# Chunk-selected attention and an MLP: scores of two heads in two halves of the PE rows, a separate mask matmul, and x centred in place of W1

## The chip, the cores and the metric

The kernel runs on one core of a Trainium2 chip. The metric is the device time of one launch in microseconds (us); lower is better. TensorE is called PE below, VectorE DVE, ScalarE ACT, GpSimd POOL and SyncE SP.

## The reference

Four batches, eight heads, 768 positions, head size 64; then a layer norm and an MLP over 512 channels with 2048 hidden ones.

```python
k_min, k_max = min and max of k over chunks of 32 positions
ub = sum over d of max(q * k_min, q * k_max)          # a bound for each query and chunk
ub = where(query's chunk >= chunk, ub, -1e9)
top_chunks = the 6 chunks with the highest ub
mask = (chunk of key in top_chunks) & (query >= key)
attn = softmax(where(mask, q @ k.T / 8, -1e9)) @ v
x = attn, heads side by side                          # 4 x 768 x 512
xn = (x - mean(x)) / sqrt(var(x) + 1e-6) * g_ln
out = x + relu(xn @ w_ch1) @ w_ch2
```

## The kernel before

**Units of work.** A pair `g` is two heads of one batch; there are 16 pairs, four to a batch. Tiles have 128 partitions; the 768 positions are six tiles. `load_qk` and `load_v` fetch a pair (q and k in f32 on SP's queue, v on POOL's, cast to f16).

**Preparation.** `prep_q` (L201) transposes q with six f32 PE transposes into a PSUM tile, casts it to f16 as `qh` on ACT, and forms the rest `ql` and the two parts `rh`, `rl` of its positive half on DVE. It copies the two heads' halves of `qh` into `QA` and `QB`. `prep_k` (L222) transposes k, takes minima and maxima over chunks on DVE, copies k on ACT into `KA` and `KB`, and builds `BD` for the bounds. `bounds` (L243) makes 20 matmuls of 96 columns, `select` (L257) finds the chunks with `max` (DVE's eight largest) and writes a 0/1 matrix `MN` of the chunks that are not selected, and `mask_t` (L274) transposes it and copies it into the other half of `QA` and `QB`.

**Scores.** The stationary operand `KA` holds 64 rows of k of one head and, in the other 64 rows, the matrix `RT`, which has -61440 where a row's chunk holds the key. `QA` has q in the same 64 rows and the transposed `MN` in the others. So one K=128 matmul (L297) gives scores and mask at once; `KB`, `QB` serve the other head with the halves exchanged. `score_bin` (L287) fills one PSUM bank `mm`, and ACT's exp (L306) empties it into `pt`. `diag` (L310) multiplies the diagonal blocks by a triangle on DVE. `values` (L317) multiplies by v with a column of ones, and `normalise` (L331) divides on DVE into `x_all`.

**MLP.** `w1_scale` multiplies W1 by the layer norm's gain, `w1_mean` computes its column means with 16 matmuls, and `w1_center` subtracts them, so that x needs no centring ahead of the product. `x_t` (L341) transposes x by pair. `stats` (L355) takes mean and variance of a row. `mlp1` (L376) and `mlp2` (L391) are the two products; the 1/std is applied at the end (L403), with the residual.

**Order.** The pieces are handed over in an order written out by hand: each has a due time `at(t, ...)` in units of one pair, and they are sorted by it (L410 to L454). The framework's scheduler then sets each engine's final queue. The MLP of a batch is spread over the four pairs that follow; that of the last batch has nothing beside it. PSUM: one two-bank `tr` tile, one `trh`, two `sm`, and three `mm` banks, which scores, W1 means and both MLP products share.

Of the kernel before, what the change touches and what calls it, by code (L numbers as in the profile page):

```python
# [9 lines left out]
ACTF = mybir.ActivationFunctionType  # L10
# [8 lines left out]
def kernel(  # L19
# [12 lines left out]

    nc = tc.nc
# [4 lines left out]
    CH = 32  # L38
    NCH = S // CH
    NT = S // P  # L40
    HP = H // 2
# [13 lines left out]
    SB0 = S - P  # L55
# [3 lines left out]
    ldp = ctx.enter_context(tc.tile_pool(name="ldp", bufs=3))  # L59
    vap = ctx.enter_context(tc.tile_pool(name="vap", bufs=4))  # L60
    prp = ctx.enter_context(tc.tile_pool(name="prp", bufs=2))
    smp = ctx.enter_context(tc.tile_pool(name="smp", bufs=2))
    ptp = ctx.enter_context(tc.tile_pool(name="ptp", bufs=3))
    xp = ctx.enter_context(tc.tile_pool(name="xp", bufs=2))
    htp = ctx.enter_context(tc.tile_pool(name="htp", bufs=1))
    outp = ctx.enter_context(tc.tile_pool(name="outp", bufs=3))

    PSUM = bass.MemoryType.PSUM
    ps_t = ctx.enter_context(tc.tile_pool(name="ps_t", bufs=1, space=PSUM))
# [4 lines left out]
    q_r = q.rearrange("b h (t p) d -> b p t h d", p=P)  # L74
    k_r = k.rearrange("b h (t p) d -> b p t h d", p=P)
    v_r = v.rearrange("b h (t p) d -> b p t h d", p=P)
    out_r = out.rearrange("b (t p) n -> b t p n", p=P)

    pieces = []

    def at(t, fn):
        pieces.append((t, len(pieces), fn))
# [4 lines left out]
    Lmask = const.tile([P, P], F16, name="Lmask", tag="Lmask")  # L87
    causb = const.tile([P, NT - 1, NCH], F32, name="causb", tag="causb")
    RT = const.tile([P, S], F16, name="RT", tag="RT")
    mean_w = const.tile([P, P], F16, name="mean_w", tag="mean_w")  # L90
    mhalf = const.tile([P, NT], F32, name="mhalf", tag="mhalf")
    NR = 3
    QA = [ring.tile([P, S], F16, name=f"QA{i}", tag=f"QA{i}") for i in range(NR)]
    QB = [ring.tile([P, S], F16, name=f"QB{i}", tag=f"QB{i}") for i in range(NR)]
    KA = [ring.tile([P, S], F16, name=f"KA{i}", tag=f"KA{i}") for i in range(NR)]
    KB = [ring.tile([P, S], F16, name=f"KB{i}", tag=f"KB{i}") for i in range(NR)]

    BD = [ring.tile([P, 2, 2, 2, NCH], F16, name=f"BD{i}", tag=f"BD{i}") for i in range(2)]
    MN = [ring.tile([P, NT - 1, P], F16, name=f"MN{i}", tag=f"MN{i}") for i in range(2)]

    def consts_first():
        make_identity(nc, ident_f)
        nc.vector.tensor_copy(ident_h, ident_f)
        for i in range(2):
            nc.vector.memset(BD[i], 0.0)
        for i in range(2):
            nc.vector.memset(MN[i], 0.0)
        nc.gpsimd.memset(causb, 0.0)
        nc.gpsimd.affine_select(
            out=causb, in_=causb, compare_op=ALU.is_ge, fill=CAUSAL,  # L110
            base=P, pattern=[[P, NT - 1], [-CH, NCH]], channel_multiplier=1,
        )
        nc.gpsimd.memset(RT, 0.0)
        for r0 in (0, 64):
            rr = RT[r0:r0 + NCH, :]
            nc.gpsimd.memset(rr, -NEGM)
            nc.gpsimd.affine_select(
                out=rr, in_=rr, compare_op=ALU.is_ge, fill=0.0,
                base=0, pattern=[[1, S]], channel_multiplier=-CH,
            )  # L120
            nc.gpsimd.affine_select(
                out=rr, in_=rr, compare_op=ALU.is_ge, fill=0.0,
                base=CH - 1, pattern=[[-1, S]], channel_multiplier=CH,
            )
        nc.gpsimd.memset(Lmask, 1.0)
        nc.gpsimd.affine_select(
            out=Lmask, in_=Lmask, compare_op=ALU.is_ge, fill=0.0,
            base=0, pattern=[[1, P]], channel_multiplier=-1,
        )
        nc.gpsimd.memset(mhalf, -0.5)  # L130
        nc.gpsimd.memset(mean_w, 1.0 / DM)

    def consts_ring(i):
        nc.vector.tensor_copy(KA[i][64:P, :], RT[64:P, :])
        nc.vector.tensor_copy(KB[i][0:64, :], RT[0:64, :])
        nc.vector.memset(QA[i][64:P, 0:P], 0.0)
        nc.vector.memset(QB[i][0:64, 0:P], 0.0)
# [5 lines left out]
    w1mean = const.tile([P, HID], F16, name="w1mean", tag="w1mean")  # L143
    w1_r = moe_w_ch1.rearrange("(kt p) n -> p kt n", p=P)
    w2_r = moe_w_ch2.rearrange("(kt p) n -> p kt n", p=P)

    def w1_load(kt):
        if kt == 0:
            nc.sync.dma_start(gstr, moe_g_ln.rearrange("(kt p) -> p kt", p=P))
        nc.gpsimd.dma_start(w1b[:, kt, :], w1_r[:, kt, :])  # L150
# [3 lines left out]

    def w1_scale(kt):
        nc.vector.tensor_scalar(
            w1b[:, kt, :], w1b[:, kt, :], gstr[:, kt:kt + 1], None, op0=ALU.mult,
        )

    def w1_mean(j):  # L160
        mp = ps_m.tile([P, 512], F32, name="mm", tag="mm")
        for kt in range(KT1):
            nc.tensor.matmul(
                mp, mean_w, w1b[:, kt, 512 * j:512 * j + 512], start=(kt == 0), stop=(kt == KT1 - 1),
            )
        nc.scalar.copy(w1mean[:, 512 * j:512 * j + 512], mp)

    def w1_center(kt):
        nc.vector.tensor_tensor(w1b[:, kt, :], w1b[:, kt, :], w1mean, ALU.subtract)  # L169
# [13 lines left out]
    def load_qk(g):  # L183
        b, hp = divmod(g, HP)
        qn = ldp.tile([P, NT, 2, D], F32, name="qn", tag="qn")
        kn = ldp.tile([P, NT, 2, D], F32, name="kn", tag="kn")
        for hh in range(2):
            nc.sync.dma_start(qn[:, :, hh, :], q_r[b, :, :, 2 * hp + hh])
        for hh in range(2):
            nc.sync.dma_start(kn[:, :, hh, :], k_r[b, :, :, 2 * hp + hh])  # L190
        st[g].update(qn=qn, kn=kn)

    def load_v(g):
        b, hp = divmod(g, HP)
        va = vap.tile([P, 2, NT, 80], F16, name="va", tag="va")
        for hh in range(2):
            nc.gpsimd.dma_start(va[:, hh, :, 0:D], v_r[b, :, :, 2 * hp + hh])  # L197
        nc.gpsimd.memset(va[:, :, :, D:D + 1], 1.0)
        st[g].update(va=va)

    def prep_q(g):  # L201
        qn = st[g]["qn"]
        pst = ps_t.tile([P, S], F32, name="tr", tag="tr")
        for t in range(NT):
            nc.tensor.transpose(pst[:, t * P:(t + 1) * P], qn[:, t, :, :], ident_f)  # L205
        qh = prp.tile([P, S], F16, name="qh", tag="qh")
        ql = prp.tile([P, SB0], F16, name="ql", tag="ql")
        rh = prp.tile([P, SB0], F16, name="rh", tag="rh")
        rl = prp.tile([P, SB0], F16, name="rl", tag="rl")
        nc.scalar.activation(qh, pst, ACTF.Copy, scale=QS)  # L210
        nc.vector.scalar_tensor_tensor(  # L211
            ql, pst[:, P:S], QS, qh[:, P:S], op0=ALU.mult, op1=ALU.subtract,
        )
        nc.vector.tensor_scalar_max(rh, qh[:, P:S], 0.0)
        nc.vector.scalar_tensor_tensor(  # L215
            rl, qh[:, P:S], 0.0, ql, op0=ALU.is_gt, op1=ALU.mult,
        )
        nc.vector.tensor_copy(QA[g % NR][0:64, :], qh[0:64, :])
        nc.vector.tensor_copy(QB[g % NR][64:P, :], qh[64:P, :])
        st[g].update(qh=qh, ql=ql, rh=rh, rl=rl)  # L220

    def prep_k(g):  # L222
        kn = st[g]["kn"]
        pst = ps_t.tile([P, S], F32, name="tr", tag="tr")
        for t in range(NT):
            nc.tensor.transpose(pst[:, t * P:(t + 1) * P], kn[:, t, :, :], ident_f)  # L226
        view = pst.rearrange("p (c e) -> p c e", e=CH)
        kc = smp.tile([P, 2, NCH], F32, name="kc", tag="kc")
        kx = smp.tile([P, NCH], F32, name="kx", tag="kx")
        nc.vector.tensor_reduce(kc[:, 0, :], view, axis=AX.X, op=ALU.min)  # L230
        nc.vector.tensor_reduce(kx, view, axis=AX.X, op=ALU.max)  # L231
        nc.scalar.copy(KA[g % NR][0:64, :], pst[0:64, :])  # L232
        nc.scalar.copy(KB[g % NR][64:P, :], pst[64:P, :])  # L233
        nc.vector.tensor_tensor(kc[:, 1, :], kx, kc[:, 0, :], ALU.subtract)
        bd = BD[g % 2]
        for r0, hh in ((64, 0), (0, 1)):
            r = slice(r0, r0 + 64)
            nc.vector.tensor_scalar(bd[r, :, 0, hh, :], kc[r], KS, None, op0=ALU.mult)
            nc.vector.scalar_tensor_tensor(  # L239
                bd[r, :, 1, hh, :], kc[r], KS, bd[r, :, 0, hh, :], op0=ALU.mult, op1=ALU.subtract,  # L240
            )

    def bounds(g):  # L243
        p, bd = st[g], BD[g % 2]
        ub = ps_s.tile([P, NT - 1, 2, 2, NCH], F32, name="sm", tag="sm")
        for s in range(NT - 1):
            o = ub[:, s].rearrange("p l h c -> p (l h c)")
            stats = [(p["qh"], P, 0), (p["ql"], 0, 0), (p["rh"], 0, 1), (p["rl"], 0, 1)]
            for i, (a, off, arr) in enumerate(stats):
                c0 = off + s * P  # L250
                nc.tensor.matmul(  # L251
# [233 lines left out]
```

## Time and profile before

| What | Value |
|---|---|
| median of 3 runs | 345.12 us (343.38 to 345.32) |
| the profiled execution's own time | 344.2 us |
| its span | 342.5 us |
| PE busy | 294.4 us (86%), 2528 matmuls |
| DVE busy | 221.3 us (65%), 645 instructions |
| ACT busy | 188.9 us (55%), 373 instructions |
| POOL busy | 46.8 us (14%), 79 instructions |
| chain that ended last | PE 63%, DVE 20%, ACT 8%, POOL 4%, DMA 3% |

The span is what the profiler records from the first to the last instruction; the profiled execution's own time is a little longer. Matmuls are pipelined and their ends are modelled, so a mean duration of a matmul is a latency, and what a full PE spends on one is the distance between starts. A group's line gives busy us and mean ns of one, then the engine's idle us just before the group and what ended it. In the 40 slices a digit is the busy share in tenths.

### The profile page before, as it was taken

The page shows a single profiled execution, that of the slowest core. Times are in us where ns is not written, and L with a number is a line of the kernel's source. Part 1 is how long each engine was busy: PE and PEld are TensorE (multiplying, and loading weights), DVE is VectorE, ACT ScalarE, POOL GpSimd, SP SyncE. Part 2 cuts the span into 40 slices and gives each one's busy share as a digit, 9 for nine tenths or more (in the row PEclk, how much of TensorE's full clock was granted, in tenths as well). Part 3 has the DMA queues.
Part 4 walks back from the last instruction along what each step waited for, and adds up shares of the span by engine and source line. Part 5 has one row for each costly group of instructions (what it writes and reads, how often), then busy time and mean ns, then how long its engine had stood idle before and what let it go on. Part 6 is the DMA issues. An engine that isn't in the chain of part 4 may idle for free.

```text
span 342.5 us, 6455 instructions
## 1 busy us (share of the span) xinstructions
PE 294.4 (86%) x2528; PEld 182.5 (53%) x2528; DVE 221.3 (65%) x645; ACT 188.9 (55%) x373; POOL 46.8 (14%) x79
## 2 busy tenths in 40 slices
PE   2226678786599999999999999998998999999995
PEld 1214456354366665656666656565665554565442
DVE  4839898999995656878965766869862543710111
ACT  2103686776387865454978764537787635166100
POOL 8940020121112020202030202020100000010000
PEclk9985898999899999999999999999999999999999
DMA  9999998582623432737152442322000011100021
GB/s 177 184 213 183 196 210 137 71 115 49 69 48 24 94 25 80 116 91 130 49 71 48 60 89 44 72 44 43 2 3 0 2 61 61 63 2 0 31 94 61
DMA packets 81966, 26.63 MB, mean 78 GB/s; under 512 B 76304, under 2 KB 78352, under 8 KB 81936
## 3 DMA queue, kind: packets, MB, share of 16 engines
q1 hardware_dynamic: 54160, 18.88, 23.9%
q0 software_dynamic: 27776, 7.34, 21.0%
q8 instruction: 20, 0.33, 0.4%
q14 instruction: 10, 0.08, 0.1%
HBM read 27.27 MB, written 6.29 MB: 98 GB/s over the span
## 4 chain that ended last, share of the span: by engine, by line
PE 63%; DVE 20%; ACT 8%; POOL 4%; DMA 3%; issue 1%; ACTq 0%; POOLq 0%
PE mm L383 22%; PE mm L396 22%; PE mm L297 7%; PE sm L326 3%; DMA w1b<-in_moe_w_ch_dram 3%; PE sm L251 3%; DVE m L268 3%; DVE ql L211 2%; ACT pt L306 2%; DVE rl L215 2%; ACT hT L387 2%; PE tr L205 2%; ACT KB L233 2%; POOL va L197 1%; ACT KA L232 1%; DVE w1b L169 1%
## 5 line engine op out<-in xcount | busy, mean ns | idle before, releaser
L306 ACT ACTIVATE pt<-mm 128x512 f16<-128x512 f32 (+1 forms) x192 | 99.5, 548 | 47.5 <-PE mm L297 46.5
L383 PE MATMUL mm<-xT,w1b 128*128 128x512 f16 (+1 forms) x512 | 98.4, 328 | 5.8 <-DVE xT L350 2.7
L396 PE MATMUL mm<-w2b,hT 128*128 128x512 f16 x384 | 93.1, 379 | 0.5 <-ACT pt L306 0.5
L387 ACT ACTIVATE hT<-mm 128x512 f16<-128x512 f32 (+1 forms) x128 | 59.8, 493 | 37.3 <-PE mm L383 37.1
L383 PEld LDWEIGHTS <-w1b 128*128 128x128 f16 x512 | 48.7, 98 | 37.0 <-issue 6.7
L396 PEld LDWEIGHTS <-hT 128*128 128x128 f16 x384 | 35.1, 97 | 33.1 <-issue 0.8
L197 POOL DMA_DIRECT2D va<-in_v_dram x32 | 27.0, 849 | 153.4 <-issue 125.8
L403 DVE SCALAR_TENSOR_TENSOR ot<-mm,rstd,x_all 128x512 f32<-128x512 f32 x24 | 17.9, 747 | 41.0 <-PE mm L396 41.0
L326 PEld LDWEIGHTS <-pt 128*128 128x128 f16 x672 | 30.4, 98 | 13.4 <-DVE pt L313 3.3
L297 PE MATMUL mm<-QA,KA 128*128 128x512 f16 (+3 forms) x128 | 33.1, 325 | 4.4 <-DVE QA L279 4.3
L313 DVE TENSOR_TENSOR pt<-pt,Lmask 128x768 f16<-128x768 f16 x32 | 17.7, 553 | 29.0 <-ACT pt L306 29.0
L326 PE MATMUL sm<-va,pt 128*128 128x65 f16 x672 | 34.5, 194 | 1.2 <-DVE pt L313 1.0
L297 PE MATMUL mm<-QB,KB 128*128 128x512 f16 (+3 forms) x128 | 32.1, 309 | 2.2 <-ACT pt L306 1.5
L205 PE MATMUL tr<-ident_f,qn 128*128 128x128 f32 x96 | 18.2, 315 | 9.0 <-DMA qn<-in_q_dram 4.8
L232 ACT CAST KA<-tr 64x768 f16<-64x768 f32 x16 | 12.6, 789 | 23.2 <-DVE kx L231 23.2
L226 PE MATMUL tr<-ident_f,kn 128*128 128x128 f32 x96 | 16.9, 292 | 9.0 <-DVE ql L211 9.0
L210 ACT ACTIVATE qh<-tr 128x768 f16<-128x768 f32 x16 | 13.1, 819 | 16.4 <-PE tr L205 16.4
L251 PE MATMUL sm<-BD,qh 128*128 128x96 f16 x80 | 15.2, 215 | 6.3 <-DVE BD L239 6.3
L261 DVE TENSOR_TENSOR ubt<-sm,causb 128x240 f32<-128x240 f32 x16 | 6.5, 407 | 21.2 <-PE sm L251 21.1
L297 PEld LDWEIGHTS <-KA 128*128 128x128 f16 x128 | 12.7, 103 | 13.8 <-DVE QA L279 4.4
L226 PEld LDWEIGHTS tr<-ident_f,kn 128*128 128x128 f32 x96 | 12.4, 151 | 13.1 <-DVE ql L211 10.1
L297 PEld LDWEIGHTS <-KB 128*128 128x128 f16 x128 | 12.4, 99 | 11.9 <-issue 3.5
(67 smaller groups left out, 361.6 us busy)
## 6 DMA issues: line engine op xcount, KB each, us to landing
qn<-in_q_dram SPq DMA_DIRECT2D x32, 192.0 KB, 3.3
kn<-in_k_dram SPq DMA_DIRECT2D x32, 192.0 KB, 4.0
out_dram<-ot SPq DMA_DIRECT2D x24, 256.0 KB, 2.0
va<-in_v_dram POOLq DMA_DIRECT2D x32, 96.0 KB, 3.6
w1b<-in_moe_w_ch_dram POOLq DMA_DIRECT2D x4, 512.0 KB, 11.4
w2b<-in_moe_w_ch_dram POOLq DMA_DIRECT2D x4, 512.0 KB, 21.1
gstr<-in_moe_g_ln_dram SPq DMA_DIRECT2D x1, 2.0 KB, 5.6
```

The lines of the kernel that those rows point to most:

```text
L197: nc.gpsimd.dma_start(va[:, hh, :, 0:D], v_r[b, :, :, 2 * hp + hh])
L205: nc.tensor.transpose(pst[:, t * P:(t + 1) * P], qn[:, t, :, :], ident_f)
L226: nc.tensor.transpose(pst[:, t * P:(t + 1) * P], kn[:, t, :, :], ident_f)
L251: nc.tensor.matmul(o, a[:, c0:c0 + P], bd[:, arr].rearrange("p l h c -> p (l h c)"), start=(i == 0), stop=(i == 3),)
L297: nc.tensor.matmul(sc[:, o:o + c1 - c0], ks[:, t * P:(t + 1) * P], qs[:, c0:c1], start=True, stop=True,)
L306: nc.scalar.activation(dst, sc[:, 0:o].rearrange("p (a c) -> p a c", a=len(segs)), ACTF.Exp, scale=SCALE / QS,)
L313: nc.vector.tensor_tensor(dv, dv, Lmask.unsqueeze(1).to_broadcast([P, NT, P]), ALU.mult,)
L326: nc.tensor.matmul(pv[:, s, 0:D + 1], flat[:, c0:c0 + P], va[:, hh, t, 0:D + 1], start=(t == 0), stop=(t == s),)
L383: nc.tensor.matmul(hp_[:, 0:cw], w1b[:, kt, m * P:(m + 1) * P], xT[:, kt, c0:c0 + cw], start=(kt == 0), stop=(kt == KT1 - 1),)
L387: nc.scalar.activation(hts[b][:, m, c0:c0 + cw], hp_[:, 0:cw], ACTF.Relu, scale=HS)
L396: nc.tensor.matmul(yp, hts[b][:, kt, s * P:(s + 1) * P], w2b[:, kt, :], start=(kt == 0), stop=(kt == KT2 - 1),)
L403: nc.vector.scalar_tensor_tensor(ot, yp, rs[b][1][:, s:s + 1], x_all[:, s].rearrange("p h d -> p (h d)"), op0=ALU.mult, op1=ALU.add,)
```

## The change

- **Scores.** `qh` and the new `kh` keep both heads of a pair, head A in rows 0 to 63 and head B in rows 64 to 127. A score matmul takes 64 rows (K=64) and leaves its accumulation open; a mask matmul of K=24 in rows 0 to 23 or 32 to 55 (a 32-row tile) adds `RT` times `mt`, the transposed selection. `QA`, `QB`, `KA`, `KB` and the copies into them are gone. A piece is now a third of the queries, for both heads: `score_bins(g, r)` has one, two or three bins per head for r = 0, 1, 2, and a bin takes two `mm` banks, one per head. The exp's columns stay the same.
- **Diagonal.** `diag` becomes one POOL `affine_select` of 512 elements per third.
- **Normalise, stats.** By thirds, with both heads in one operation; `bn_stats` runs on 128 channels of a pair, and `bn_aggr` joins four of them.
- **MLP.** W1 is neither scaled nor centred. `centre` subtracts the mean from x into `xc` on DVE, `x_t` transposes `xc` for a whole batch, four channel blocks of six transposes, and its copy out of PSUM multiplies by the gain.
- **Preparation.** q and k are transposed in pieces of two tiles through two one-bank `tr` buffers; `prep_b` builds `BD` of both heads at once with `hsel`.
- **Loads.** The q/k ring has four slots (three before), v five (four). W1 and W2 are due earlier; `w_gate` writes one element of the weight tile from `kc` of a later pair, so that the load of block 0 waits for that pair's chunk minima. `gstr` comes on ACT's queue.
- **Order.** The due times are new; the pairs of batches 1 to 3 start `GAP` = 1.5 units later than they would without it, and the MLP of batch 0 is spread over that time too.

```diff
-        qn = ldp.tile([P, NT, 2, D], F32, name="qn", tag="qn")
...
+    def turn(g, nm, t0, t1):
+        pst = ps_t.tile([P, 512], F32, name="tr", tag="tr")
+        src = st[g][nm]
+        for t in range(t0, t1):
+            nc.tensor.transpose(pst[:, (t - t0) * P:(t - t0 + 1) * P], src[:, t, :, :], ident_f)
+        return pst[:, 0:(t1 - t0) * P]
...
-        nc.vector.tensor_copy(QA[g % NR][0:64, :], qh[0:64, :])
-        nc.vector.tensor_copy(QB[g % NR][64:P, :], qh[64:P, :])
...
-        nc.scalar.copy(KA[g % NR][0:64, :], pst[0:64, :])
-        nc.scalar.copy(KB[g % NR][64:P, :], pst[64:P, :])
+        nc.scalar.copy(st[g]["kh"][:, c], pst)
...
+    def w_gate(w, g):
+        nc.gpsimd.tensor_copy(w[0:1, 0, 0:1], st[g]["kc"][0:1, 0, 0:1])
...
+    def prep_b(g):
+        kc, bd = st[g]["kc"], BD[g % NK]
+        km = smp.tile([P, 2, 2, NCH], F32, name="km", tag="km")
+        nc.vector.tensor_tensor(kc[:, 1], kc[:, 1], kc[:, 0], ALU.subtract)
+        nc.vector.tensor_tensor(
+            km, kc.unsqueeze(2).to_broadcast([P, 2, 2, NCH]),
+            hsel.unsqueeze(1).unsqueeze(3).to_broadcast([P, 2, 2, NCH]), ALU.mult,
+        )
+        nc.vector.tensor_copy(bd[:, :, 0], km)
+        nc.vector.tensor_tensor(bd[:, :, 1], km, bd[:, :, 0], ALU.subtract)
...
+    def score_bins(g, r):
+        nb = 4 * r + 3
+        pt = st[g]["pt", r] = ptp.tile([P, nb, 2, P], F16, name=f"pt{r}", tag=f"pt{r}")
+        qh, kh, mt = st[g]["qh"], st[g]["kh"], st[g]["mt"]
+        segs = [(2 * r + 1, 2 * r + 1, 1), (2 * r, 2 * r, 2)] + [(t, 2 * r, 2) for t in range(2 * r)]
+        done = 0
+        while segs:
+            sc = [ps_m.tile([P, 512], F32, name="mm", tag="mm") for _ in range(2)]
+            o = 0
+            here = []
+            while segs and o + segs[0][2] * P <= 512:
+                t, s, w = segs.pop(0)
+                here.append((o, t, s, w))
+                o += w * P
+            for o1, t, s, w in here:
+                for hh in range(2):
+                    row = slice(64 * hh, 64 * hh + 64)
+                    nc.tensor.matmul(
+                        sc[hh][:, o1:o1 + w * P], kh[row, t * P:(t + 1) * P],
+                        qh[row, s * P:(s + w) * P], start=(o1 == 0), stop=False,
+                    )
+            masked = [(o1 + P * (s == 0), t, max(s, 1), w - (s == 0)) for o1, t, s, w in here if s + w > 1]
+            for o1, t, s, w in masked:
+                for hh in range(2):
+                    row = slice(32 * hh, 32 * hh + NCH)
+                    nc.tensor.matmul(
+                        sc[hh][:, o1:o1 + w * P], RT[row, t * P:(t + 1) * P],
+                        mt[row, s * P:(s + w) * P], start=False, stop=(o1 == masked[-1][0]),
+                    )
+            for hh in range(2):
+                nc.scalar.activation(
+                    pt[:, done:done + o // P, hh, :],
+                    sc[hh][:, 0:o].rearrange("p (n x) -> p n x", x=P),
+                    ACTF.Exp, scale=SCALE / QS,
+                )
+            done += o // P
+
+    def diag(g, r):
+        dv = st[g]["pt", r][:, 0:2].rearrange("p n h x -> p (n h) x")
+        nc.gpsimd.affine_select(
+            out=dv, in_=dv, compare_op=ALU.is_ge, fill=0.0,
+            base=0, pattern=[[0, 4], [1, P]], channel_multiplier=-1,
+        )
...
+    def centre(b, t0, t1):
+        x_all, _ = xb(b)
+        r = rs[b]
+        for s in range(t0, t1):
+            nc.vector.bn_aggr(r["mv"][:, s, :], r["st"][:, s])
+            nc.vector.tensor_scalar(
+                r["xc"][:, s, :], x_all[:, s].rearrange("p h d -> p (h d)"),
+                r["mv"][:, s, 0:1], None, op0=ALU.subtract,
+            )
...
+    def x_t(b, kt, t0, t1):
+        _, xT = xb(b)
+        px = ps_h.tile([P, S], F16, name="trh", tag="trh")
+        for s in range(t0, t1):
+            nc.tensor.transpose(
+                px[:, (s - t0) * P:(s - t0 + 1) * P], rs[b]["xc"][:, s, kt * P:(kt + 1) * P], ident_h,
+            )
+        nc.vector.tensor_scalar(
+            xT[:, kt, t0 * P:t1 * P], px[:, 0:(t1 - t0) * P], gstr[:, kt:kt + 1], None, op0=ALU.mult,
+        )
...
+    GAP = 1.5
+    for g in range(NG):
+        T = float(g - HP) + (GAP if g >= HP else 0.0)
+        at(T - 2.8 if g > 3 else -8 + 0.1 * g, load_qk, g, 0, NR)
+        at(T - 2.6 if g else T - 3.2, load_v, g, 0, NT)
...
+        at(T - 1.3, prep_b, g)
+        at(T - 0.98, bounds, g, 0, NT)
+        at(T - 0.97, select, g, 0, NT, n_sel)
+        at(T - 0.45, mask_t, g, 0, NT, n_sel)
+        for r in range(NR):
+            at(T + 0.3 * r, score_bins, g, r)
+            at(T + 0.3 * r + 0.3, diag, g, r)
+            at(T + 0.3 * r + 0.4, values, g, r)
+            at(T + 0.3 * r + 0.45, normalise, g, r)
+            at(T + 0.3 * r + 0.47, stats, g, 2 * r, 2 * r + 2)
+    at(-4.5, w_gate, w1b, 1)
+    at(-2.9, w_gate, w2b, 3)
+    for kt in range(KT1):
+        at(-4.4 + 0.01 * kt, w1_load, kt)
+        at(-2.8 + 0.01 * kt, w2_load, kt)
+    for b in range(B):
+        e = 4.0 * b + (GAP if b > 0 else 0.0)
...
+        for kt in range(KT1):
+            at(e + 0.10 + 0.01 * kt, x_t, b, kt, 0, NT)
+        at(e + 0.2, rstd, b, 0, NT)
+        e = e + 0.15
+        d = 4.0 * (b + 1) + GAP + 0.15 - e
+        if b == B - 1:
+            d = 4.0
+        for n in range(32):
+            c0, cw = ((0, 512), (512, 256))[n % 2]
+            at(e + 0.05 + 0.5 * d * n / 32, mlp1, b, (n // 2,), c0, cw)
+        for n in range(24):
+            at(e + 0.06 + 0.5 * d + 0.5 * d * n / 24, mlp2, b, n // 4, n % 4)
```

## The prediction

> **What bounds the kernel now.** I began with the page's 40 slices, because a mean over the span hides that this kernel has stages.
>
> ```profile
> PE   2226678786599999999999999998998999999995
> DVE  4839898999995656878965766869862543710111
> DMA  9999998582623432737152442322000011100021
> ```
>
> VectorE (DVE) is full in slices 6 to 12, where TensorE (PE) is not; from slice 12 on PE is full. The first MLP matmul starts at 91.74 us in the chain, so I asked for the windows before and behind that point (columns: length, then busy us and instructions of PE, weight loads, DVE, ACT, POOL; clock; DMA).
>
> ```profile
> 0.00:40.00 40.00, 15.95 (x97) 11.95 (x97) 25.72 (x78) 12.06 (x20) 19.57 (x39) 0.83 1.29 190
> 40.00:91.70 51.70, 37.15 (x433) 24.68 (x434) 48.78 (x144) 32.52 (x62) 7.37 (x12) 0.96 0.78 118
> 91.70:296.70 205.00, 199.66 (x1777) 124.21 (x1775) 137.88 (x407) 130.36 (x261) 18.56 (x27) 0.99 0.29 54
> 296.70:338.40 41.70, 41.61 (x224) 21.72 (x222) 8.19 (x20) 13.96 (x32) 1.32 (x1) 1.00 0.10 39
> ```
>
> Until 91.7 us DVE is the bound: 48.8 of 51.7 us in the second window. In the first it also idles, and the waits of DVE name the cause (engine and line, waited for: total, times, longest):
>
> ```profile
> DVE w1b L156 <- DMA w1b<-in_moe_w_ch_dram: 7.0, 2, 5.9
> DVE ql L211 <- ACT qh L210: 6.1, 5, 3.9
> ```
>
> The scaling of W1 stands in DVE's queue ahead of attention work and waits there for the weights. After 91.7 us PE is the bound, 241.3 busy us in 246.7. So the span is 91.7 (DVE) + 246.6 (PE, to 338.35) + 4.1 (last `ot` and its store) = 342.5 us; the profiled run took 344.2 us, 1.7 more, and is 0.9 below the median of 345.12.
>
> The prices come from the groups by shape, the chain and ACT's timeline:
>
> ```profile
> L211 DVE SCALAR_TENSOR_TENSOR ql<-tr,qh 128x640 f16<-128x640 f32 x16 | 13.1, 821 | 6.4 <-ACT qh L210 6.1
> L230 DVE TENSOR_REDUCE kc<-tr 128x24 f32<-128x768 f32 x16 | 15.3, 954 | 1.8 <-PE tr L226 1.8
> L337 DVE TENSOR_TENSOR x_all<-sm,rden 128x384 f16<-128x384 f32 x32 | 17.6, 550 | 0.4
> L364 DVE BATCH_NORM_STATS2 st<-x_all 128x6 f32<-128x512 f16 x24 | 15.6, 676 | 0.0
> L156 DVE TENSOR_SCALAR w1b<-w1b,gstr 128x2048 f16<-128x2048 f16 x4 | 3.0, 746 | 7.0 <-DMA w1b<-in_moe_w_ch_dram 7.0
> L169 DVE TENSOR_TENSOR w1b<-w1b,w1mean 128x2048 f16<-128x2048 f16 x4 | 4.8, 1202 | 0.0
> L251 PE MATMUL sm<-BD,qh 128*128 128x96 f16 x80 | 15.2, 215 | 6.3 <-DVE BD L239 6.3
> ```
> ```profile
> 296.68 20.92 PE mm L383 x128
> 317.59 20.73 PE mm L396 x96
> ```
> ```profile
> 282.63 0.98 ACT L306 ACTIVATE pt<-mm 128x512 f16<-128x512 f32 x2 [0.82 <-PE mm L297]
> 290.44 0.77 ACT L306 ACTIVATE pt<-mm 128x384 f16<-128x384 f32 x2 [0.76 <-PE mm L297]
> ```
>
> A matmul's 379 ns is latency; its price on a full PE is 20.73/96 = 216 ns for 512 columns, 0.42 ns a column. Exps in a row come every 0.49 us (512 columns) and 0.385 us (384).
>
> **The first stage.** DVE loses 3.0 + 4.8 = 7.8 us of W1 work and the 7.0 us wait for it. Per head pair: the pieces of `ql`, `rl` cost 0.06 + 1.19 ns an element, so 0.94 us each instead of 0.82; `rh` 0.48 (0.35); six reduces of 256 instead of two of 768, 2.15 (1.90); `prep_b`, four small operations by the 180 to 203 ns of the old ones and a width of 96, 0.88 (0.95); select 2.2, unchanged; QA/QB copies 0.78, gone; one mask copy 0.49 instead of 0.98; diagonal mask 1.1, moved to POOL; three normalises of 256 at 0.39 plus reciprocals at 0.18, 1.71 (1.47); six `bn_stats` of 128 at 0.21, 1.28 (1.26 spread). Sum 11.1 us a pair, against 13.2 before without the output operation. The built order of the changed program puts in front of the first xT copy four pairs (44.3), centring (6 x 0.42 = 2.5), the preparation of pair 4 (6.2) and constants (1.7): 54.7 us. To it come 4.9 us until the first q has landed (PE waits 4.82 us for it now), about 6% idle as in the second window (3.4), and 5.5 us for the first pair's chain across ACT and PE and for the last exps: 68.5 us instead of 91.7. Bounds: 61 with no other idle time, 80 with the 17.2 idle us of now plus a late start. POOL's 48 diagonal masks (512 wide; the 768-wide select of now takes 816 ns, so 0.56) and ACT's three pieces (386 ns each, 1.16 us instead of 0.82 for q and 1.58 for k) lie beside DVE; if POOL's cover were gone, 48 x 0.56 = 27 us. The gates put waits into POOL's queue: behind them stand two W1 loads, `va` of pair 3, and W2 loads. These transfers are wanted tens of us later, so I give them nothing; late `va` would hold `values` and is within the upper bound. SP issues the same 64 loads, four ring slots deep instead of three, and gstr moves to ACT's queue.
>
> **The scores.** Before, 12 of the 16 pairs' score columns lie behind the first MLP matmul: 62464 columns, 26.0 us. The changed program has there 288 K=64 matmuls of 64512 columns and 288 mask matmuls of 61440: in series 52.5 us, 4.37 a pair. If each pair of heads ran truly together it would be 26.2. No row here shows a matmul in part of the rows, so both ends are open. Going through the built order, many pairs are not adjacent (two of head A, its masks, then head B); overlapping only neighbours in different rows leaves 40.8 us. And the scores now come in bursts: a bin takes two of the three `mm` banks at once, and the last third of a pair has six bins with little between them. ACT frees banks every 0.39 to 0.49 us. Following the six-bin burst by hand, PE needs 2.65 us if serial and 2.35 if paired; four-bin burst 1.63 or 1.38; two-bin 0.53 or 0.40: 4.8 or 4.1 a pair. What pairing gains is mostly spent waiting for ACT. I take 4.5, 54 us.
>
> A change of row layout may also empty the array. The program has 318 such changes behind the first MLP matmul. Lower bound nothing; upper bound the latency that the 96-column row shows beyond its spacing, 0.215 - 0.043 = 0.17 us, 55 us in all. I take nothing extra, since much of it would fall into waits for ACT, and keep a third (18 us) in the range.
>
> The Trainium skill speaks both ways. "TensorE: Matmul & The Clock Gate", Part 3, says that matmuls in different row groups run together, with 3.07x for four K=32 tiles of 512 columns; by it the scores would go towards 26 us and the time towards 326. "TensorEngine Tiling (Array Packing)" says under Key Properties that changing the tiling mode drains TensorE, and under PSUM Bottleneck that tiling does not speed up evacuation. The first page puts the drain near 128 cycles, as an estimate 318 x 53 ns = 17 us, which would make 371. No run here shows either yet.
>
> **The rest of the PE stage.** Transposes: 12 more f32 ones behind the line (0.11 us each, 0.47 for four in the chain), less 21 value matmuls: +1.1. Four x transposes now come together at each MLP start with one buffer: transposes 0.34, DVE copy 0.55, handovers, 1.2 us a step against some 0.9 of other PE work: about 1 us a batch, +4 (bounds 0 and 10). W1's 16 mean matmuls lay in the first stage, under DVE: no gain on PE.
>
> Sum: 68.5 + (246.6 - 26.0 + 54 + 1.1 + 4 = 279.7) + 4.1 + 1.7 = 354.0 us. The change wins 23 us where DVE was the bound and gives 33 back where PE is.
>
> **The rivals.**
> - Tiles overlap well, also across the two layouts, and ACT keeps up. For it: the stage has 130 us of ACT in 205. Against: bursts. Scores 36 us: 336; fully paired 326. This is the faster side; it decides below about 41 us of scores.
> - Every change of layout empties the array for a good part of the 0.17 us: 354 + 20 to 30 = 374 to 384. For it: 0.17 us is real latency on every short matmul. Against: nothing in this trace, which has one layout throughout; the waits for ACT would hide a part.
> - The first stage doesn't shrink, because chains across PE, ACT and POOL with finer pieces leave DVE idle: 80 us instead of 68.5, 365. Against: 94% busy now once the weights are out of the way.
>
> **How the numbers follow.** Forecast 0.43 (its own range 344 to 363), well-overlapped tiles 0.27, drains 0.16, first stage 0.14. The predicted time is 354. The range goes from 332 to 375: down into the overlapped case, up through the third of the drains. One per cent is about what a measurement of this kernel can tell. Faster by over 1% (under 341.7 us) is the overlapped case with a quick first stage: 0.27; within 1%: the forecast's low end, 0.10; slower: 0.63.
>
> **What would show it.** First MLP matmul at 66 to 71 us; then 270 to 290 us to the end; waits of PE for the exps, above all inside bursts, growing from 2.1 us in this stage (`mm` L383 1.6, L396 0.5) to some 10 or more; starts of neighbouring score matmuls in different rows about 0.1 us apart for 256 columns if serial, near together if paired. Score stretches of 3 us a pair or less, or an MLP start after 76 us, would prove me wrong.

## The result, and the profile after

The changed kernel takes 416.68 us (412.64 to 420.24, four runs), the kernel before 344.28 us in the same runs: a ratio of 1.200, 95% interval 1.192 to 1.208. The forecast was 354.0, with a range of 332 to 375; the two fastest runs, 412.64 and 413.56, lie 59 us above the forecast and 38 above the range. The two other runs are 1.7 to 1.8% above the fastest and are left out of the ratio. The profiled execution took 412.64 us (span 410.9) and stands against 344.2 before: 68.4 us more.

The page's slices of the changed kernel:

```profile
PE   1639999979999999997999999998999999979995
DVE  3736564468376485877226374769344433440021
PEclk9999965567999999997599999999999999999999
```

DVE is no longer full anywhere, as the change meant; PE is, from slice 4 on. The third row is the granted clock: it stands at 0.5 to 0.7 of full in slices 6 to 10, and dips again in 19 and 20. The windows, cut at the first MLP matmul, now at 95.8 us (length, then busy us and instructions of PE, weight loads, DVE, ACT, POOL; clock; DMA):

```profile
0.00:50.00 50.00, 31.52 (x214) 18.15 (x214) 25.51 (x109) 14.73 (x34) 21.82 (x44) 1.00 1.28 186
50.00:95.70 45.70, 42.92 (x345) 22.68 (x345) 26.86 (x119) 21.49 (x47) 11.75 (x18) 0.58 0.57 84
95.70:369.00 273.30, 264.55 (x2271) 142.60 (x2269) 151.40 (x589) 137.71 (x309) 39.79 (x60) 0.96 0.22 44
369.00:406.80 37.80, 37.73 (x202) 19.41 (x199) 3.78 (x6) 11.91 (x28) 0.00 (x0) 1.00 0.10 36
```

In the second window PE is busy 42.9 of 45.7 us and DVE 26.9: the first stage is bound by PE, at a mean clock of 0.58. From the first MLP matmul to the last it is 311.0 us (95.8 to 406.8); before it was 257.0 (81.3 to 338.3). So 14.5 us were lost ahead of the MLP and 54.0 behind its start.

The groups of the scores and of their masks:

```profile
L294 PE MATMUL mm<-qh,kh 64*128 64x256 f16 (+1 forms) x384 | 63.6, 287 | 1.4 <-ACT pt L307 0.2
L302 PE MATMUL mm<-mt,RT 24*128 24x256 f16 (+1 forms) x384 | 57.0, 281 | 0.0
L302 PEld LDWEIGHTS <-RT 24*128 24x128 f16 x384 | 16.5, 95 | 32.9 <-issue 32.8
```

The score matmuls wait 0.2 us in all for the exps: there is no burst that ACT holds up. What the time is spent on shows in PE's timeline (start, duration, engine and line, count), at full clock, with nothing else in between:

```profile
335.87 0.38 PE L294 MATMUL mm<-qh,kh 64*128 64x256 f16 x2
336.18 0.39 PE L302 MATMUL mm<-mt,RT 24*128 24x256 f16 x2
336.50 0.39 PE L294 MATMUL mm<-qh,kh 64*128 64x256 f16 x2
336.82 0.39 PE L302 MATMUL mm<-mt,RT 24*128 24x256 f16 x2
```

Each row is two matmuls of 256 columns, one after the other (the second starts 0.11 to 0.12 us behind the first). Their columns take 2 x 0.107 = 0.213 us (0.417 ns a column), but the rows start 0.32 us apart. The other 0.107 us is lost at each step from 64-row to 24-row matmuls or back.

The first stage shows in the 96-column bounds matmuls, which have one shape everywhere and so serve as a clock. In the kernel before, they came every 0.043 us from 45.8 us on. Now:

```profile
47.87 0.28 PE L236 MATMUL sm<-BD,ql 128*128 128x96 f16 x1
47.95 0.28 PE L236 MATMUL sm<-BD,rh 128*128 128x96 f16 x1
48.03 0.28 PE L236 MATMUL sm<-BD,rl 128*128 128x96 f16 x1
```

0.08 us apart is half speed, and it stays so at 64 us (0.079) and at 93.5 us (0.083); only at 110.7 us is it 0.043. The clock row says 1.00 for the first 50 us, though the spacing there is 0.08 already. The row knows changes only; until the first one it can't be read. That first change is a rise at 50.2 us, and the clock falls again at 53.6, though PE doesn't wait in between:

```profile
50.20:53.60 3.40, 3.40 (x34) 1.00 1.45 212
53.60:57.00 3.40, 3.40 (x16) 0.50 1.14 227
```

### The profile page after: what moved, and what is told of

The parts are those of the page before. It is cut to its first block, busy times and chain, and to the rows that moved or that the text cites. A ratio compares the mean times of both kernels' runs of the same rounds, so it can differ in the third digit from the quotient of the medians.

```text
span 410.9 us, 7765 instructions
## 1 busy us (share of the span) xinstructions
PE 376.7 (92%) x3024; PEld 202.8 (49%) x3024; DVE 208.3 (51%) x820; ACT 185.8 (45%) x417; POOL 73.4 (18%) x122
## 4 chain that ended last, share of the span: by engine, by line
PE 82%; DVE 7%; DMA 5%; SPq 2%; ACT 2%; issue 1%; ACTq 0%
PE mm L406 21%; PE mm L422 19%; PE mm L294 13%; PE mm L302 11%; PE sm L330 6%; PE tr L184 6%; DMA kn<-in_k_dram 5%; PE sm L236 4%; SPq L163 2%; PE trh L268 2%; PE trh L389 2%; DVE xc L370 1%; DVE xT L392 1%; ACT hT L410 1%; ACT pt L307 1%; DVE m L256 1%
## 5 line engine op out<-in xcount | busy, mean ns | idle before, releaser
L410 ACT ACTIVATE hT<-mm 128x512 f16<-128x512 f32 (+1 forms) x128 | 58.8, 490 | 43.7 <-PE mm L406 42.9
L316 POOL TENSOR_SCALAR_AFFINE_SELECT pt<-pt 128x512 f16<-128x512 f16 x48 | 30.6, 638 | 209.6 <-ACT pt L307 209.1
L294 PE MATMUL mm<-qh,kh 64*128 64x256 f16 (+1 forms) x384 | 63.6, 287 | 1.4 <-ACT pt L307 0.2
L302 PE MATMUL mm<-mt,RT 24*128 24x256 f16 (+1 forms) x384 | 57.0, 281 | 0.0
L340 DVE RECIPROCAL rden<-sm 128x4 f32<-128x4 f32 x48 | 8.6, 180 | 89.4 <-PE sm L330 89.4
L184 PE MATMUL tr<-ident_f,kn 128*128 128x128 f32 x96 | 24.2, 337 | 16.5 <-ACT kh L216 8.3
L294 PEld LDWEIGHTS <-kh 64*128 64x128 f16 x384 | 19.2, 97 | 36.9 <-issue 31.8
L196 ACT ACTIVATE qh<-tr 128x256 f16<-128x256 f32 x48 | 18.5, 386 | 33.9 <-PE tr L184 33.9
L302 PEld LDWEIGHTS <-RT 24*128 24x128 f16 x384 | 16.5, 95 | 32.9 <-issue 32.8
L214 DVE TENSOR_REDUCE kc<-tr 128x8 f32<-128x256 f32 x48 | 20.0, 416 | 21.6 <-PE tr L184 21.2
L216 ACT CAST kh<-tr 128x256 f16<-128x256 f32 x48 | 17.9, 373 | 24.7 <-DVE kc L215 24.6
L175 POOL DMA_DIRECT2D va<-in_v_dram x32 | 26.9, 846 | 1.1
L184 PEld LDWEIGHTS tr<-ident_f,kn 128*128 128x128 f32 x96 | 13.0, 164 | 24.6 <-ACT kh L216 10.4
## 6 DMA issues: line engine op xcount, KB each, us to landing
w1b<-in_moe_w_ch_dram POOLq DMA_DIRECT2D x4, 512.0 KB, 10.4
```

Source lines behind the costliest of these rows:

```text
L175: nc.gpsimd.dma_start(va[:, hh, t0:t1, 0:D], v[b, 2 * hp + hh, t0 * P:t1 * P, :].rearrange("(t p) d -> p t d", p=P),)
L184: nc.tensor.transpose(pst[:, (t - t0) * P:(t - t0 + 1) * P], src[:, t, :, :], ident_f)
L196: nc.scalar.activation(qh[:, c], pst, ACTF.Copy, scale=QS)
L214: nc.vector.tensor_reduce(kc[:, 0, n], view, axis=AX.X, op=ALU.min)
L294: nc.tensor.matmul(sc[hh][:, o1:o1 + w * P], kh[row, t * P:(t + 1) * P], qh[row, s * P:(s + w) * P], start=(o1 == 0), stop=False,)
L302: nc.tensor.matmul(sc[hh][:, o1:o1 + w * P], RT[row, t * P:(t + 1) * P], mt[row, s * P:(s + w) * P], start=False, stop=(o1 == masked[-1][0]),)
```

## The experiments

All times are device times; ratios are against the kernel before, run on the same chip.

**e1: the disputed costs by themselves.** Stretches of matmuls only, on W1 and W2 as data, each behind 60 full-row matmuls of 512 columns; the time of the whole means nothing.

```python
only_a:    mm(0, 64, 256)                              # one head's rows
paired64:  mm(0, 64, 256); mm(64, 64, 256)             # A B A B
twos64:    two of mm(0, 64, 256), two of mm(64, 64, 256)   # A A B B
paired24:  mm(0, 24, 256); mm(32, 24, 256)
mixed:     4 of paired64's, then 4 of paired24's
switch:    mm(0, 128, 256); mm(0, 64, 256)
```

Two more stretches, of full rows with 256 and with 65 columns, serve for comparison.

> This kernel has only matmuls of random f16 data in nine stretches, with 60 full ones of 512 columns between them to bring the clock back; the attention and the MLP are left out. It measures three disputed prices by themselves. Theory 1 (a change of row layout has a fixed price): the changed kernel's trace has two matmuls of 64 rows and 256 columns, then masks, starting 0.32 us apart where their columns need 0.21, so 0.107 us a change. Then the stretch that alternates a full and a half-row matmul of 256 columns takes 2 x 0.107 for columns and 2 x 0.107 for changes, 0.43 us for two; the stretch that goes four K=64, four K=24 takes 0.107 x 2 + 0.107 x 2 + 0.21 = 0.64 us for eight. Theory 2 (the clock gate follows the rows in use): the granted clock falls to about 0.5 in the stretches of 64 or 24 rows of about 15 to 30 us, and stays at 1.0 in the full-row stretch of 256 columns. Rival (the clock fell because of waits and short matmuls in the kernel, not because of rows): the clock stays at 1.0 in every stretch, for no stretch waits. Pairing: neighbours in different rows come two in 0.107 us if they run together, two in 0.213 if not; two of A, two of B in a row come four in 0.32 us if only neighbours overlap.

Windows inside the stretches only_a, paired64, twos64, paired24, mixed and switch (length, PE busy and instructions, clock, DMA):

```profile
80.00:100.00 20.00, 20.00 (x185) 1.00 0.00 1
130.00:140.00 10.00, 10.00 (x188) 1.00 0.01 3
160.00:168.00 8.00, 8.00 (x152) 1.00 0.01 2
200.00:215.00 15.00, 15.00 (x144) 0.50 0.00 1
245.00:265.00 20.00, 20.00 (x250) 1.00 0.00 1
300.00:350.00 50.00, 50.00 (x154) 0.50 0.00 0
```

One head's rows: 0.108 us for 256 columns (20.00/185), the same as full rows. Two heads in two halves: 0.053 each, so they do run fully together, and in the order A A B B as well (8.0/152 = 0.053), better than expected. Mixed: eight matmuls in 0.64 us; the paired columns need 0.427, and two changes of layout share the rest, (0.64 - 0.427)/2 = 0.107 us. Switch: two matmuls in 0.65 us at half clock, (0.65 - 0.427)/2 = 0.11. The change costs about the same at both clocks. 24-row pairs and switch fell to half clock, 4.6 and 5.0 us behind their first matmul, although PE never waits; 64-row stretches, of one head too (213 matmuls in 23 us), did not, against the expectation. The Trainium skill says in "TensorEngine Tiling (Array Packing)", Key Properties, that a change of tiling mode drains TensorE; these runs agree, and price it at some 0.11 us.

**e2: masks in the scores' layout.** The changed kernel, but its mask matmuls take all 64 rows of the head's half, with zeros in the unused ones. The masks' transposes write 128 columns instead of 64, so that their layout is that of the others too. Matmuls and the columns of scores and masks stay; layout changes fall from 424 (106 ahead of the first MLP matmul, 318 behind) to 194 (50 and 144) in the built order.

```diff
-                    row = slice(32 * hh, 32 * hh + NCH)
+                    row = slice(64 * hh, 64 * hh + 64)
```

> The mask matmuls take all 64 rows of their head's half (24 rows of the mask and 40 of zeros), so that scores and masks share one row layout, and the transposed selection is 128 rows high; columns, instructions and results are the same. In the built order the changes of row layout fall from 424 to 194. Theory 1 (0.107 us a change): 230 x 0.107 = 25 us less, some 388 us, with the clock still half in the first 100 us. Theory 2 (clock follows rows in use) adds up to 10 us more if 24 rows weigh less than 64: 378. Rival (the loss comes from the new schedule, its bank waits and its late transfers): no change, 410 to 418.

375.57 us, 1.089 (1.083 to 1.094): 37 us of the 68 come back with 230 changes of layout. PE's timeline shows the step itself:

```profile
300.09 0.38 PE L295 MATMUL mm<-qh,kh 64*128 64x256 f16 x2
300.31 0.38 PE L303 MATMUL mm<-mt,RT 64*128 64x256 f16 x2
300.58 0.38 PE L295 MATMUL mm<-qh,kh 64*128 64x256 f16 x2
300.79 0.38 PE L303 MATMUL mm<-mt,RT 64*128 64x256 f16 x2
```

Score to mask is now 0.22 us, the columns alone, instead of 0.32 (the step from mask to score takes 0.27 here). PE's busy time behind the first MLP matmul, in windows of both kernels over the same 2469 matmuls:

```profile
95.80:406.80 311.00, 302.18 (x2469) 0.97 0.21 43
```
```profile
76.50:369.80 293.30, 282.57 (x2469) 0.98 0.22 45
```

It fell by 19.6 us; 174 fewer changes at 0.107 are 18.6. Ahead of it the MLP starts at 76.5 us instead of 95.8, while 56 changes are worth 6 us: the rest goes with the clock, since the bounds matmuls of this kernel come every 0.043 us at 54.5 us.

**e3: one K=128 matmul again.** The changed order, thirds, POOL mask and centring of x, but scores and mask by one full-row matmul with `QA`, `QB`, `KA`, `KB`. No change of layout is left.

```diff
-                        sc[hh][:, o1:o1 + w * P], kh[row, t * P:(t + 1) * P],
-                        qh[row, s * P:(s + w) * P], start=(o1 == 0), stop=False,
...
+                        sc[hh][:, o1:o1 + w * P], ks[hh][:, t * P:(t + 1) * P],
+                        qs[hh][:, s * P:(s + w) * P], start=(o1 == 0), stop=(o1 == here[-1][0]),
```

> Undoes the score part alone: one K=128 matmul gives scores and mask as in the kernel before, with the copies into QA, QB, KA, KB, inside the changed schedule, with x centred, the diagonal on POOL, pieces by thirds and bins of two banks. No change of row layout is left. Theories 1 and 2 together: the layout changes (45 us) and the halved clock go, the first MLP matmul comes at some 75 us instead of 95.7, the rest takes 250 to 258 us, 331 to 340 us in all: faster than the kernel before. Theory 1 alone, with the clock still halved in the first stage: 350 to 360. Rival (the schedule, not the rows): it stays above 380.

354.72 us, 1.026 (1.021 to 1.032). The window behind the first MLP matmul:

```profile
73.70:349.60 275.90, 260.74 (x2181) 0.98 0.23 48
```

288 matmuls fewer, 41.4 us less of PE than in the changed kernel. The score part alone makes the difference between 1.200 and 1.026. The score matmuls wait 2.8 us in all for the exps here, so without changes of layout too ACT holds up little.

**e4: W1 centred again.** e3 with `w1_scale`, `w1_mean`, `w1_center` and `x_t` by pair, as before the change, in place of `centre`.

```diff
-            at(e + 0.10 + 0.01 * kt, x_t, b, kt, 0, NT)
+        at(T + 1.09, x_t, g)
+        at(-2.45 + 0.3 * kt, w1_scale, kt)
...
```

> Undoes a second part on top of the K=128 scores: W1 is scaled and centred again (four scalings, 16 mean matmuls, four subtractions), x isn't centred, and each pair's x is transposed by itself. What is left of the change is its schedule, its pieces and loads, and the diagonal on POOL. Theory (four dependent x transposes at each MLP start hold PE, and the clock falls behind the hole): the three holes of 2.2 to 2.6 us and the lowered clock behind them in the run with K=128 scores go, 10 to 13 us less behind the first MLP matmul; DVE's 7.8 us of W1 work come back ahead of it; 346 to 352 in all against 354.7. Rival (the finer pieces on DVE and the bins of two banks hold PE): the stage behind the first MLP matmul stays near 276 us and the time goes up by W1's work, to some 360.

345.6 us over ten runs, 1.003 (1.000 to 1.005), a little below what was expected: what is left of the change, the thirds, the POOL mask, the loads and the new order, is together worth nothing either way. Its two stages differ all the same: the first MLP matmul comes at 67.6 us instead of 81.3 in the kernel before, and the stage from there to the last one takes 270.9 us instead of 257.0, with 12 us more of PE's busy time. So the relief of DVE did shorten the first stage, and PE gave the gain back behind it.

Centring x costs 8 to 9 us (354.72 - 345.6, or 2.4% by the two ratios). Between the profiled runs of e3 and e4 6.1 us lie ahead of the first MLP matmul (73.7 against 67.6) and 4.9 behind it (275.8 against 270.9), where 10 to 13 were expected. In e3 centring shows as holes at each batch's border:

```profile
155.36 0.23 PE L392 MATMUL trh<-ident_h,xc 128*128 128x128 f16 x1 [0.79 <-DVE xc L373]
157.19 0.73 PE L392 MATMUL trh<-ident_h,xc 128*128 128x128 f16 x6 [1.60 <-DVE xT L395]
```

With one `trh` buffer each block of transposes waits for DVE's copy of the block ahead (0.62 us here). In the changed kernel the hole is 2.9 us long and stands at a q/k transpose that waits behind the same DVE queue; the clock row dips just behind it (slices 19 and 20):

```profile
188.50 0.44 PE L184 MATMUL tr<-ident_f,kn 128*128 128x128 f32 x2 [2.93 <-ACT kh L216]
```

**e5: gates that hold every block.** In the changed kernel `w_gate` holds the load of block 0 alone, and two of the other W1 loads pass it: they are issued at 9.2 and 9.8 us, the gate writes at 16.2. That is the time when q and k of the first pairs are due. The chain of the changed kernel has this piece, and PE's timeline the wait:

```profile
10.68 18.54 DMA kn<-in_k_dram
```
```profile
29.35 0.45 PE L184 MATMUL tr<-ident_f,kn 128*128 128x128 f32 x1 [6.64 <-DMA kn<-in_k_dram]
```

```diff
-        nc.gpsimd.tensor_copy(w[0:1, 0, 0:1], st[g]["kc"][0:1, 0, 0:1])
+        for j in range(4):
+            jj = j if w is w1b else 4 * j
+            nc.gpsimd.tensor_copy(w[0:1, jj, 0:1], st[g]["kc"][0:1, 0, 0:1])
```

> The changed kernel, but the gate writes one element of each of the four blocks of W1 (and W2), so that no block passes it. In the changed kernel two W1 blocks were issued ahead of the gate, and PE then waited 6.6 us for the k of a later pair, which took 18.5 us to land. Theory (weights that pass the gate delay q and k): that wait goes, and 3 to 7 us with it, 406 to 410 by one look. Rival (PE at half clock is the bound of the first stage, the wait is made up): the wait goes but the time stays within 2 us of 412.6.

One run: 407.48 us. The longest wait for `kn` is 1.1 us instead of 6.6, and the MLP starts at 88.0 instead of 95.8. It is a single run beside 412.64, so its 5 us are a size and not an interval.

**e6: the gate alone, in the kernel before.** This is the one piece of the change that looked as if it could pay.

```diff
+    def w_gate(w, step, g):
+        for kt in range(4):
+            nc.gpsimd.tensor_copy(w[0:1, step * kt, 0:1], st[g]["kc"][0:1, 0, 0:1])
...
+    at(-0.59, lambda: w_gate(w1b, 1, 1))
+    at(0.59, lambda: w_gate(w2b, 4, 2))
...
-        at(-0.6 + 0.25 * kt, lambda kt=kt: w1_load(kt))
+        at(-0.58 + 0.01 * kt, lambda kt=kt: w1_load(kt))
```

> The kernel before with one thing added: a gate ahead of the four W1 loads (an element of each block written from the chunk minima of pair 1) and of the W2 loads (pair 2). DVE then has the W1 scaling later in its queue and doesn't wait 7.0 us for the weights ahead of attention work. Theory: 5 to 8 us less, 337 to 340. Rival (the wait only moves: DVE needs the weights all the same, later): no change, 343 to 346.

339.81 us, 0.987 (0.983 to 0.991): 1.3% below the kernel before, and less than both kernels. W1 starts only when the chunk minima of pair 1 are there, is issued 9.8 us later, and its last block lands at 37.1 us instead of 29.7; but it takes less from issue to landing (median 8.6 us instead of 11.4; W2 10.6 instead of 21.1), and k of pair 3 has landed at 22.5 us instead of 32.8. DVE's wait for W1, 7.0 us before, is now

```profile
DVE w1b L160 <- DMA w1b<-in_moe_w_ch_dram: 0.9, 1, 0.9
```

and the MLP starts at 77.0 us instead of 81.3. How much comes from that wait and how much from the earlier q and k wasn't separated.

**e7: what raises the clock.** Matmuls only again: `mixed` from the cold start, then `full512`, `paired24` (to lower the clock), `mixed`, `full512`, `paired24`, `paired64`; behind these `full512`, `paired24`, `switch`, `twos64`, `full512`.

> Matmuls alone, as in the first such kernel; attention and MLP are left out. It asks what lifts the clock from half: stretches of mixed K=64 and K=24 matmuls with layout changes, of paired K=64 ones, and of K=64 ones after changes at each matmul, each behind a stretch that holds the clock low (the first at the very start). Theory (the gate weighs rows in use times the time in which they stream; K=24 pairs with 48 of 128 rows brought it to 0.5, the mix kept it at 1.0): the paired K=64 stretch lifts the clock within some us; the mix, at half clock with 0.43 of each 1.07 us... in 128 rows and 0.43 in 48, that is 55% of the array, lifts it too. Rival (layout changes or K=24 keep a cold array cold, though they don't cool a warm one): the mix stays at half clock from a cold start, 8 matmuls in 1.07 us instead of 0.64; this is what the changed kernel's first 95 us look like.

Windows in the first `mixed`, in the second, and in `paired64`:

```profile
90.00:100.00 10.00, 10.00 (x76) 1.00 0.00 0
160.00:170.00 10.00, 10.00 (x76) 0.50 0.01 2
310.00:320.00 10.00, 10.00 (x172) 0.91 0.01 2
320.00:330.00 10.00, 10.00 (x188) 1.00 0.02 3
```

In e1 the mixture ran at full clock for 31 us, 125 matmuls in 10 us. Here it makes 76, from the start to 100 us (where the row again shows 1.00, no change having come yet) and from 160 to 265 us. 64-row pairs raise the clock within 4 us (from 308.1 us on, the clock rises at 311.8), and `twos64` within 2; `switch` stays at half. So the theory fell and the rival holds: this mixture neither lowers a full clock nor raises a half one.

**e8: a push.** The changed kernel with 28 matmuls that no result needs.

```diff
+            if (g, r, done) == (0, 2, 0):
+                for _ in range(28):
+                    nc.tensor.matmul(sc[0], qh[:, 0:P], qh[:, 0:512], start=True, stop=True)
```

> The changed kernel with 28 more matmuls of 128 rows and 512 columns (qh by qh of pair 0, about 37 us into the span, into the bank of pair 0's third group of bins, whose first score matmul then starts over it): work that no result needs. The question is whether the half clock of the first stage is a state in which the mixture of 128-, 64- and 24-row matmuls merely stays, since it does not raise a cold clock. My theory: it stays where it is put. The 28 matmuls cost about 10 us (19 at 0.43, the rest at 0.22), raise the clock within some 8 us, and the mixture then holds it: the bounds matmuls behind them come every 0.043 us instead of 0.079, the 45 us of PE time other than layout changes that follow at half clock take some 22, the first MLP matmul comes at 80 to 86 us instead of 95.8, and the time falls to 396 to 404 us although the work grew. Rival: the 24-row matmuls cool the array again within some 10 us, as the stretch of 24-row pairs did: the spacing is back at 0.079 before 65 us, the MLP starts at 100 to 106, and the time is 418 to 424. Second rival: the clock is kept down by the first stage's PE waits and not by rows; then it rises in this kernel only while the 28 run, same as the first rival.

404.51 us (399.08 to 406.47, four runs), below the fastest run of the changed kernel, with more work. PE's timeline and the windows ahead of the 28, during them and behind:

```profile
36.52 1.90 PE L287 MATMUL mm<-qh 128*128 128x512 f16 x4
...
41.15 4.49 PE L287 MATMUL mm<-qh 128*128 128x512 f16 x20
```
```profile
30.00:37.00 7.00, 7.00 (x48) 1.00 1.22 196
37.00:45.60 8.60, 8.60 (x37) 1.00 1.36 193
45.60:70.00 24.40, 24.40 (x324) 1.00 0.92 137
```

The first four take 0.42 us each (1.69 us to the next row), the last twenty 0.22: the clock rose within 5 us. It stays up: 324 instructions in the next 24.4 us, 13 a microsecond against 8 in the changed kernel's 50 to 70 us, and the bounds matmuls at 62 us come every 0.043 us. The MLP starts at 85.5 us instead of 95.8, though the 28 took 8 us. Both rivals, by which the clock falls again within some 10 us or as soon as the 28 are done, are out. But the kernel doesn't hold the clock for good. At 75.2 us it falls, with 0.03 us of waits in the 6.8 us ahead of that, and at 83 us, behind the first holes for `centre`, the spacing is 0.08 again:

```profile
68.40:75.20 6.80, 6.77 (x85) 1.00 0.47 33
75.20:78.60 3.40, 2.77 (x39) 0.50 0.00 0
```

## Why the prediction was wrong

**The two stages.** The prediction's sum was 68.5 + 279.7 + 4.1 + 1.7. Measured: 95.8 + 311.0 + 4.1 + 1.7 = 412.6. Both large terms failed, by 27.3 and 31.3 us.

**"I take nothing extra" for the changes of layout.** This step failed first. The bounds, 0 and 0.17 us each, held the truth: 0.107 us, 34 us for the 318 behind the first MLP matmul. The reason for taking the lower bound, "much of it would fall into waits for ACT", was wrong, because those waits don't exist (0.2 us in the whole run). The estimate from the skill's page in the prediction was half of the measured price. The rival of the drains had the right mechanism, and 20 to 30 us for it.

**"What pairing gains is mostly spent waiting for ACT."** Wrong for the same reason: the banks were followed by hand without the time that the changes take, and with it PE is too slow to be held up. By PE's busy time, e3's 260.7 us contain the scores as 64512 full-row columns, 26.9 us; the changed kernel's 302.2 us therefore contain 26.9 + 41.4 = 68.3 us for scores, masks and changes of layout, against the 54 predicted. Less 34 for changes, 34.3 us are left for columns that would take 52.5 in series (e2 gives 33.3 in the same way): pairing did work, between the two bounds of 26.2 and 40.8 that were given for it. It paid 18 us and the changes took 34.

**The first stage, 68.5 us.** DVE's part was right: DVE is off the bound, and with the scores in full rows and W1 centred again (e4) the MLP does start at 67.6 us. The term that was missing is PE's. PE was taken to be free there, since it was busy 37 of 52 us before; it wasn't asked what PE's work costs if the clock stays at half. e8 gives the size: pushed up at 37 us, the stage is 10.3 us shorter although 8 us of work were added, so some 18 us. The wait for k behind W1's loads, to which the prediction gave nothing ("I give them nothing" of the gates), is the other part: 6.6 us, or 7.8 us of MLP start by e5. The 106 changes of layout ahead of the MLP, 11 us of PE's time, lie in the same stage. The three overlap and can't simply be added to the 27 us: with 56 changes fewer and the clock up sooner, e2 starts its MLP 19 us earlier. The low prices of DVE's short pieces (256-wide reduce 0.358 predicted, 0.416 measured; its 128-channel statistics 0.214 and 0.284) mattered little, since PE was the bound.

**The border.** The prediction took 91.74 us, the first MLP matmul on the chain, for the first one there is. The first lies at 81.3, and the stage from there took 257.0 us, not 246.6. The 10.4 us between, 6.6 of PE's work (247.9 busy us instead of 241.3; 13 of the matmuls are the MLP's, the others attention's) and 3.8 of waits, were lost from the second term.

**Centring, "about 1 us a batch, +4".** By e3 and e4 the 4.9 us behind the first MLP matmul are near the 4 predicted; the other 6.1 lie in the first stage, where the prediction had 2.5 us for it, and this although e4 has W1's work on DVE back there. The cost consists of the holes and of what the clock loses behind them; their shares weren't separated.

The 31.3 us of the second term are then 14.3 for scores and changes of layout, 10.4 for the border, and about 7 by the clock: a mean of 0.97 over 311 us is 6% of it at half, some 9 us lost, against 2.6 at 0.99 before. These parts overlap a little, since the 14.3 hold some of what the clock took, and the 7 is an estimate. Seen by parts of the change, the runs give 68.4 = 37 (masks in another layout, with what the clock adds) + 21 (two matmuls in place of one; the 194 changes of layout that e2 still has are 20.8 us at 0.107) + 9 (centring x) + 1 (order and loads).

## What to carry to other kernels

Row tiles that run together pay only while the layout stays the same: count the changes of layout in the built order and charge each with 0.11 us, a quarter of a full 512-column matmul at half clock and half of one at full. If a small operand can be padded with zeros to the layout of its neighbours, as in e2, it costs its columns and nothing else. A stage in which PE looks idle can have no spare PE time if its clock is at half: read the spacing of one short matmul of fixed shape through the stage before you move a bound to PE.

## What the runs showed of the hardware

- A change of layout (64 rows, 24-row tiles, full rows) costs 0.107 us at full clock, the same in the kernel and in e1, and about 0.11 at half.
- Matmuls in two halves of the rows overlap fully in the order A B A B and in A A B B: 0.053 us for 256 columns.
- The clock fell to half under an array that never waited: within 4.5 to 6.1 us of 24-row pairs (e1, e7), and within 5.0 us of alternating layouts. The mixture of e1 and e7 kept whichever clock it found, 31 us at full (e1), 100 us at half (e7); the changed kernel, whose share of 24-row work varies, rose and fell by itself. The Trainium skill, "TensorE: Matmul & The Clock Gate", Part 1, tells of a throttle that a busy window of about 3.4 us releases; here PE was busy 10.00 of 10 us for 100 us at half clock, so the measurement stands against it for small row tiles.
- One measure fits all stretches: rows in use times the share of the time in which columns stream, where a column at half clock counts half. It is 0.38 for 24-row pairs and for the switch at full clock (both fell), 0.46 for the mixture and 0.5 for one head's 64 rows at full clock (neither fell), 0.27 for the mixture at half (not raised) and 0.5 for 64-row pairs at half (raised).
- The same measure, counted through all ten profiles, separates the two clocks at 0.385. The clock records change only on a grid of 3.41 us. Behind a step of this grid with 0.385 or more the clock was full, behind one with less it was half, in 1114 of 1118 steps and in 83 of the 85 changes (f32 transposes count twice, as 128 of their columns take 0.11 us). In the changed kernel the step from 46.8 us has 0.41, and the clock rises at 50.2; the next has 0.29, without a wait, and the clock falls at 53.6. This measure was fitted to the runs afterwards, and no run was made to test it; what the gate itself counts stays open.
